# First queries by a cast load on GpSimd, bias differences from two loads, values by cast loads

## The chip, the cores and the metric

The kernel runs on one core of a Trainium2 chip. A core has a matmul engine (TensorE, PE in the profile; its weight loads are PEld), a vector engine (VectorE, DVE), a scalar engine (ScalarE, ACT), GpSimd (POOL) and a sync engine (SyncE, SP) that here only issues DMAs. Each engine works off its own instructions in order and waits on semaphores for the others. DMAs issued by SP and ACT go to hardware queues (q1 and q10 in the profile), those issued by POOL to a software queue (q0). A DMA that changes the type on its way (a cast load) is issued by POOL here. The metric is the time of one execution on the device in microseconds; lower is better.

## What is computed

Attention with a relative position bias, for 8 batch elements, 8 heads, 576 positions and head size 64, followed by a layer with two matmuls and a sine between them:

```python
scores = scale * np.matmul(q, k.transpose(0, 1, 3, 2))     # scale = 1/8
bias = bias_table[bucket]                                  # bucket of |i - j|, 32 buckets, 8 heads
scores = scores + bias.transpose(2, 0, 1)[None, :, :, :]
attn = softmax(scores)
x = np.matmul(attn, v)          # to (4608, 512), heads side by side
h = x @ w_in                    # (512, 2048)
g = h + np.sin(alpha * h) ** 2 / (alpha + 1e-09)
out = g @ w_out                 # (2048, 512)
```

Buckets of all distances of 128 and more share the last bucket. The bias table has 32 rows, one column a head.

## The kernel before

**Stages.** The batch elements are the index t, 0 to 7. For each t the kernel first does attention: score units on TensorE, exponentials on ScalarE, the bias as a product on VectorE, products with the values on TensorE, a normalisation on VectorE and a transpose into xT. Then comes the layer: matmuls with w_in, sines on ScalarE, squares on ScalarE or VectorE, g on VectorE, and matmuls with w_out, which are used later as fill between the score units of the next t. ScalarE loads a table of functions for the exponentials and another for the sines (ACT_TABLE_LOAD); the second load of the span marks the end of the first element's exponentials, the third the end of its sines.

**Bias.** The bias enters as a factor: exp(scores/8) is multiplied by exp(bias - last bias), with the last bucket's bias subtracted, so that far distances need no product. `less_last`, a 32x32 matrix that comes along in the constant `phi_x`, forms the differences by a product with the table `tabN` on TensorE (line 510). ScalarE takes the exponential (`tabE`, line 512), and `plan_table` spreads it over the distances by a product with `phi_sb`, copies the row to `e_sb` (line 595), writes it five times to DRAM (`e_dram`, line 596) and reads it back shifted by one element a partition as `m2r` (line 470) and `mhr` (line 477). The loads of `m2r` and `mhr` are issued by SP, in order, the first of them once `e_dram` has landed.

**Score units.** An attention element is four pairs of heads p, worked in two groups g. For t = 0 a pair has five units: four of kind A (128 keys by 512 queries and two heads, `ex` at line 678 with 128x1024 elements) and one of kind C (the last 64 keys of both heads, 128x576). Each takes two of TensorE's eight accumulation banks; three such pairs of banks are in use. For A units VectorE multiplies the part near the diagonal by `m2r` (line 703), for C units VectorE or GpSimd by `mhr` (line 687). Products with the values (`plan_av`) are groups of nine matmuls with one column more than the values, which gives the sum for the normalisation (lines 885 and 886). Its result is transposed by TensorE (line 910) or by a DMA, and copied to `xT`.

**First keys and queries.** For t = 0 keys and queries come from the inputs and are transposed by TensorE. Pair 0 comes by two SP loads in 32 bits (`nat0`, lines 489 and 490), is cast into `natb` by VectorE (keys, line 464), ScalarE and GpSimd (queries, lines 515 and 516), and takes six transposes of 96x128 each for keys and queries (line 550). Pairs 1 to 3 come by cast loads of GpSimd (`load_pair`, `nat1`) and take twelve transposes of 96x64 each (line 556). VectorE copies all of them to `kT` and `qT` (line 539), and GpSimd copies the last 64 keys to `kt` (line 581). For t = 1 all heads come by two cast loads (`loads2`, `nat2`), later elements from a staged copy by DMA transposes.

**First values.** Heads 0, 1 and 4 to 7 come by SP loads in 32 bits into the space of `w_out` (`load_v32`, line 416) and are cast by GpSimd (`cast_v`, line 419); heads 2 and 3 by cast loads (`load_vh`, line 411). The last 64 positions of all heads come by `load_vt`. The loads of `w_in` are issued by GpSimd behind `cast_v(4)`.

**Filler matmuls.** `warm` and `warm1` put matmuls on zeros (`zz`) onto TensorE, eight with 512 columns at the start, and shorter ones behind transposes and score units (`pad`) and in planned gaps. Their result is not used.

**Order.** The instructions ahead of `Plan` stand in the order of the code. Everything else is a task with its possible engines, an assumed cost on each, what it depends on, a priority, and in places a time before which it is not planned (the constants `T_...`). `Plan.run` places the tasks in assumed time before the launch and so writes each engine's order out; the chip then only waits on semaphores. A change of a constant can therefore move instructions far from it.

Of the kernel before, what the change touches and what calls it, by code (L numbers as in the profile page):

```python
# [209 lines left out]
WARM_END = 22.0  # L210
# [7 lines left out]
T_WI = 16.7  # L218
T_E = 5.9
T_CL = 20.5  # L220
T_FIRST = (5.2, 6.3)
T_PAIR = ((7.0, 7.4), (8.8, 9.4), (11.0, 11.6))
T_ACT = ()
T_M2 = (13.0, 14.5, 16.0, 16.0)
T_MH = 15.8
T_RST = 25.0
T_V0 = (7.5, 8.2, 8.9, 9.6)
T_VA = (10.5, 11.0)
T_VB = (16.3, 17.8, 18.3, 18.8)
T_AL = (20.0, 100)  # L230
# [4 lines left out]
NORM0 = 1200  # L235
SQ = {"ACT": 0.52, "DVE": 0.38}
T_V = ((15.5, 19.0), (50.0, 50.0))
T_TR1 = (36.5, 38.0)
T_W = (25.5, 30.5)
T_WO = (41.0, 43.5, 46.5, 49.5)  # L240
WARM0 = 8
WARM1 = 5
WARM_LAG = 0.3
WARM_GAP = 0.12
WARM_FROM = 7.3
# [19 lines left out]
def kernel(  # L265
# [41 lines left out]
    for x in range(EW - 1):  # L307
        phi_np[bt[abs(x - 255)], x] = 1.0
    last_np = np.eye(NB, dtype=np.float32)
    last_np[NB - 1] -= 1.0  # L310
    phi_h = nc.inline_tensor(np.concatenate([phi_np, last_np.view(np.float16)], axis=1), "phi_const")
# [24 lines left out]
    phi_x = sgl.tile([NB, EW + 2 * NB], F16, name="phi_sb")  # L336
    phi_sb, less_last = phi_x[:, 0:EW], phi_x[:, EW : EW + 2 * NB].bitcast(F32)
# [10 lines left out]
    N0 = 2 * 2 * SI * D  # L348
    nat0 = natx[0:SN, 0 : 2 * N0].bitcast(F32).rearrange("s (kq h x) -> s kq h x", kq=2, h=2)
    natb = natx[0:SN, 2 * N0 : 3 * N0].rearrange(  # L350
        "s (kq i two d) -> s kq i two d", kq=2, i=SI, two=2
    )
# [110 lines left out]
    def cast0(kq, eng):  # L463
        eng.tensor_copy(
            out=natb[:, kq], in_=nat0[:, kq].rearrange("s two (i d) -> s i two d", i=SI)
        )

# [15 lines left out]
    P_ = nc.gpsimd  # L483
    P_.memset(id_sb, 1.0)
# [4 lines left out]
    load_nat(nat0[:, 0], 0, 2, k[0], nc.sync)  # L489
    load_nat(nat0[:, 1], 0, 2, q[0], nc.sync)  # L490
    nc.scalar.dma_start(out=tabN, in_=bias_table)
    nc.scalar.dma_start(out=phi_x, in_=phi_h.ap())
    nc.scalar.dma_start(out=alphaN, in_=moe_alpha.rearrange("(f p) -> f p", p=128))
    load_v32(0)
    load_v32(1)
# [7 lines left out]
    load_pair(2)  # L503
    P_.tensor_copy(out=idf_sb, in_=id_sb[0:NF, 0:NF])
# [3 lines left out]
    for _ in range(WARM1):  # L508
        warm1(7, 192)
    full(pb[0:NB, 1, 0:H], less_last, tabN, True, True)  # L510
    warm1(7, 192)
    nc.scalar.activation(out=tabE, in_=pb[0:NB, 1, 0:H], func=AF.Exp)
    cast0(0, nc.vector)
    x0 = nat0[:, 1].rearrange("s two (i d) -> s i two d", i=SI)
    nc.scalar.activation(out=natb[:, 1, :, 0], in_=x0[:, :, 0], func=AF.Copy)
    P_.tensor_copy(out=natb[:, 1, :, 1], in_=x0[:, :, 1])

# [23 lines left out]
    def plan_tr(t, p, kq, pri, nb, deps=()):  # L541
# [3 lines left out]
        def mm(e):  # L545
            c.v = bank(b).bitcast(F16)
            for i in range(SI):
                x = i * SN
                if t == 0 and p == 0:
                    nc.tensor.transpose(  # L550
                        out=c.v[:, x : x + SN], in_=natb[:, kq, i], identity=id_sb[0:SN, 0:SN]
                    )
                    continue
                for z in range(2):
                    h = 2 * p - 2 + z if t == 0 else 2 * p + z
                    nc.tensor.transpose(
                        out=c.v[64 * z : 64 * z + 64, x : x + SN],
                        in_=(nat1 if t == 0 else nat2)[:, kq, h, D * i : D * i + D],
                        identity=id_sb[0:SN, 0:SN],
                    )  # L560
# [8 lines left out]
        if t == 0:  # L569
            m.pad = (256,) if p else (192,) * (5 if kq else 1)  # L570
        eng = {"DVE": 0.75, "ACT": 0.6}
        if t == 0:
            eng = {"ACT": 0.65} if p in T_ACT and kq else {"DVE": 0.75}
# [13 lines left out]
    def plan_table():  # L587
# [6 lines left out]
        def cp(e):  # L594
            nc.scalar.activation(out=e_sb, in_=bank(b)[0:H, 0:EW], func=AF.Copy)
            nc.scalar.dma_start(
# [11 lines left out]
        plan.add({"ACT": 1.0}, cp, [x], -1100, use=[b])  # L608
# [498 lines left out]
```

## Time and profile before

| | |
|---|---|
| median of 3 runs | 382.89 us (382.48 to 382.98) |
| profiled execution | 383.65 us |
| its span, first to last instruction | 381.8 us |
| mean granted TensorE clock | 0.991 |
| TensorE busy | 373.5 us, 98% of the span |
| ScalarE busy | 313.5 us, 82% |
| VectorE busy | 266.9 us, 70% |
| table load after the first element's exponentials | at 30.77 us |
| table load after the first element's sines | at 50.39 us |

The profile is of one execution, and times in it count from the start of its span. Durations below are from it; the median is of other executions of the same kernel. A row of the chain of waits has a start, a length, and an engine with what it writes and the line, or DMA with what it moves. A row of the timeline has a start, a duration, the engine, the line, the operation and its operands; for a DMA it is the time to issue it, and its landing is told apart. [...]

### The profile page before, as it was taken

The numbers are of one execution on the slowest core, as the hardware profiler recorded it, in microseconds if no ns is written. First come the engines' busy times: TensorE is split into PE (matmuls) and PEld (weight loads), VectorE is DVE, ScalarE is ACT, GpSimd is POOL, SyncE is SP. The second block draws the span as 40 slices with busy tenths as digits, with TensorE's granted clock in tenths as the row PEclk, the third lists the DMA queues.
The fourth block names the chain that finished last, engine by engine and source line by source line (L and its number), as shares of the span: only waits on it lengthen the run. The fifth ranks groups of instructions, "written<-read, shape, count | busy, mean of one in ns | idle before, by whom it ended". The sixth has DMA issues, their size and how long they took to land.

```text
span 381.8 us, 8975 instructions
## 1 busy us (share of the span) xinstructions
PE 373.5 (98%) x3578; PEld 204.2 (53%) x3578; DVE 266.9 (70%) x590; ACT 313.5 (82%) x432; POOL 92.9 (24%) x136
## 2 busy tenths in 40 slices
PE   8899999999999999999999999999999999999995
PEld 4365445654465445785564456544677456444442
DVE  4496976769676967697668867796769676999000
ACT  2978999869997999799987999699979997998111
POOL 7477350046000550037000900073005000000000
PEclk9979999999999999999999999999999999999999
DMA  9989999299912999279927991699629522000212
GB/s 170 177 160 196 203 154 134 56 162 116 89 53 74 151 120 121 79 130 113 137 60 123 103 165 44 105 147 139 78 75 155 60 53 74 6 2 1 77 63 82
DMA packets 148106, 40.16 MB, mean 105 GB/s; under 512 B 136200, under 2 KB 142432, under 8 KB 148064
## 3 DMA queue, kind: packets, MB, share of 16 engines
q0 software_dynamic: 96032, 17.67, 57.3%
q1 hardware_dynamic: 51856, 21.84, 25.1%
q8 instruction: 28, 0.46, 0.5%
q14 instruction: 14, 0.11, 0.1%
q10 hardware_dynamic: 176, 0.09, 0.1%
HBM read 37.73 MB, written 16.56 MB: 142 GB/s over the span
## 4 chain that ended last, share of the span: by engine, by line
PE 89%; ACT 5%; DMA 2%; DVE 2%; issue 1%; ACTq 0%; DVEq 0%; SPq 0%
PE pb L454 89%; ACT s L950 2%; DMA m2r<-e_dram 1%; ACT u L678 1%; DMA e_dram<-e_sb 1%; ACT sq L957 1%; PE pb L910 1%; ACT qT L537 0%; DVE u L703 0%; DVE xn L886 0%; DVE sq L959 0%; DVE outs L539 0%; DVE kT L539 0%; DVE g L964 0%; ACT xT L537 0%
## 5 line engine op out<-in xcount | busy, mean ns | idle before, releaser
L678 ACT ACTIVATE u<-pb 128x1024 f16<-128x1024 f32 (+1 forms) x174 | 152.7, 962 | 12.8 <-PE pb L454 12.0
L454 PE MATMUL pb<-w_out,g 128*128 128x512 f16 x576 | 138.9, 380 | 0.2 <-DVE outs L539 0.2
L454 PE MATMUL pb<-xT,w_in 128*128 128x512 f16 (+4 forms) x704 | 127.7, 340 | 0.0
L950 ACT ACTIVATE s<-pb,alphaT 128x512 f16<-128x512 f32 x144 | 92.9, 685 | 15.4 <-PE pb L454 15.2
L964 DVE SCALAR_TENSOR_TENSOR g<-sq,inv_a,pb 128x512 f16<-128x512 f16 x144 | 101.3, 743 | 3.8 <-ACT sq L957 2.3
L454 PEld LDWEIGHTS <-w_in 128*128 128x128 f16 x704 | 64.1, 98 | 55.9
L703 DVE TENSOR_TENSOR u<-u,m2r 128x512 f16<-128x512 f16 (+1 forms) x128 | 62.4, 497 | 35.0 <-ACT u L678 31.4
L454 PEld LDWEIGHTS <-g 128*128 128x128 f16 x576 | 53.0, 98 | 60.1 <-issue 8.1
L454 PEld LDWEIGHTS <-u 128*128 128x128 f16 x1404 | 55.5, 99 | 10.9 <-issue 3.2
L454 PE MATMUL pb<-v,u 128*128 128x65 f16 x1248 | 55.3, 195 | 0.2 <-DVE u L703 0.2
L399 POOL COPY kt<-kT 64x256 f16<-64x256 f16 x12 | 5.6, 464 | 182.9 <-DMA kT<-staged_k 182.7
L454 PE MATMUL pb<-qT,kT 64*128 64x64 f16 (+1 forms) x512 | 42.8, 288 | 0.4 <-ACT u L678 0.2
L959 DVE TENSOR_TENSOR sq<-s 128x512 f16<-128x512 f16 x81 | 34.3, 425 | 11.1 <-ACT s L950 10.2
L957 ACT ACTIVATE sq<-s 128x512 f16<-128x512 f16 x63 | 39.8, 631 | 0.9
L454 PE MATMUL pb<-vh,u 128*128 128x130 f16 x156 | 34.9, 224 | 0.0
L886 DVE TENSOR_TENSOR xn<-pb,rd 128x256 f16<-128x256 f32 (+1 forms) x64 | 30.9, 482 | 2.4 <-DVE rd L885 0.3
L537 ACT ACTIVATE outs<-pb 128x512 f32<-128x512 f32 x15 | 9.0, 597 | 28.1 <-PE pb L454 28.1
L454 PEld LDWEIGHTS <-kT 64*128 64x128 f16 x512 | 16.7, 94 | 24.5 <-issue 16.6
L404 POOL DMA_DIRECT2D v<-in_v_dram x28 | 24.8, 898 | 4.7 <-DMA nat<-in_q_dram 2.4
L1025 ACT ACT_TABLE_LOAD x15 | 19.2, 1283 | 0.3
L885 DVE RECIPROCAL rd<-pb 128x4 f32<-128x4 f32 (+1 forms) x64 | 11.9, 185 | 10.8 <-PE pb L454 9.7
L539 DVE COPY outs<-pb 128x512 f32<-128x512 f32 x21 | 14.5, 689 | 4.1 <-PE pb L454 4.0
(77 smaller groups left out, 168.7 us busy)
## 6 DMA issues: line engine op xcount, KB each, us to landing
out_dram<-outs SPq DMA_DIRECT2D x36, 256.0 KB, 2.3
v<-in_v_dram POOLq DMA_DIRECT2D x28, 128.0 KB, 4.4
staged_k<-in_k_dram POOLq DMA_DIRECT2D x6, 576.0 KB, 8.2
staged_q<-in_q_dram POOLq DMA_DIRECT2D x6, 576.0 KB, 12.0
w_in<-in_moe_w_in_dram POOLq DMA_DIRECT2D x4, 512.0 KB, 7.8
w_out<-in_moe_w_out_dram POOLq DMA_DIRECT2D x4, 512.0 KB, 15.1
xT<-xn SPq DMA_TRANSPOSE x60, 2.3
w_out<-in_v_dram SPq DMA_DIRECT2D x6, 128.0 KB, 4.8
```

Source lines behind the costliest of these rows:

```text
L404: nc.gpsimd.dma_start(out=vs[t % 2][:, c, :, 0:D], in_=vp[128 * c : 128 * c + 128],)
L454: nc.tensor.matmul(out=out, lhsT=lhsT, rhs=rhs, start=start, stop=stop)
L539: k_of(e).tensor_copy(out=o, in_=i)
L678: nc.scalar.activation(out=o, in_=x, func=AF.Exp, scale=0.125)
L703: nc.vector.tensor_tensor(out=io, in0=io, in1=m2[:, 2 * p : 2 * p + 2, x0 : x0 + hi - lo], op=ALU.mult)
L885: nc.vector.reciprocal(out=r, in_=x[:, :, :, D])
L886: nc.vector.tensor_tensor(out=xn.v[:, 0:nq].rearrange("p c (z d) -> p c z d", z=2), in0=x[:, :, :, 0:D], in1=r.unsqueeze(3).to_broadcast([ ...
L950: nc.scalar.activation(out=s16.v, in_=h.v, func=AF.Sin, scale=alphaT[:, f : f + 1])
L957: nc.scalar.activation(out=sq.v, in_=s16.v, func=AF.Square)
L959: k_of(e).tensor_tensor(out=sq.v, in0=s16.v, in1=s16.v, op=ALU.mult)
L964: nc.vector.scalar_tensor_tensor(out=gcell[b].v[:, f, :], in0=sq.v, scalar=inv_a[:, f : f + 1], in1=h.v, op0=ALU.mult, op1=ALU.add,)
L1025: nc.scalar.preload_act_table_set(name)
```

## The change

- The queries of pair 0 come by a cast load into `natq`, the first instruction of GpSimd, ahead of the identity matrix. They are transposed in twelve 96x64 pieces like the later pairs, without casts. The keys of pair 0 keep their SP load and VectorE's cast, now as the only cast. All three later pairs are loaded straight behind on GpSimd.
- The table's last row is loaded a second time, repeated over 32 partitions (`tabL`); VectorE subtracts, ahead of the key cast in its order. The constant holds `phi` alone, and the product with `less_last` and the five fillers ahead of it are gone. `phi` is now the first load on ScalarE's queue, `tabL` the second, `alphaN` the third; `tabN` is SP's second load.
- `e_dram` is written by a DMA of SP instead of ScalarE.
- The values of heads 0 to 3 all come by cast loads; `load_v32(0)`, `load_v32(1)` and their casts are gone.
- Copies of the queries of pairs 0 and 3 are ScalarE's (`T_ACT`), the first ahead of the first exponential, the second behind the seventh. The transpose of alpha stands behind the first score unit, and its three VectorE operations right behind.
- The multiply by `mhr` of pair 1 moves to VectorE, four copies of xT of the first element from ScalarE to VectorE. GpSimd's clearing of the second buffers moves behind the loads of `nat2` and `w_out`.
- With the planned times the order of score units, products and transposes of the first element changes: transposes of later pairs stand between the first score units, and the first product stands behind the eleventh score unit instead of the twelfth. There are 21 fillers instead of 40. From the second element on, the instructions are the same, in nearly the same order.

The core of the diff:

```diff
-WARM_END = 22.0
+WARM_END = 20.0
...
-T_E = 5.9
...
-T_FIRST = (5.2, 6.3)
-T_PAIR = ((7.0, 7.4), (8.8, 9.4), (11.0, 11.6))
-T_ACT = ()
-T_M2 = (13.0, 14.5, 16.0, 16.0)
-T_MH = 15.8
...
+T_E = 4.75
...
+T_FIRST = (5.0, 5.4)
+T_PAIR = ((7.4, 8.1), (8.8, 9.5), (10.2, 10.9))
+T_M2 = (11.8, 13.0, 14.4, 14.4)
+T_MH = 12.8
+T_ACT = (0, 3)
...
-WARM1 = 5
-WARM_LAG = 0.3
+WARM_LAG = 0.8
...
-    phi_h = nc.inline_tensor(np.concatenate([phi_np, last_np.view(np.float16)], axis=1), "phi_const")
+    phi_h = nc.inline_tensor(phi_np, "phi_const")
...
     P_ = nc.gpsimd
+    load_nat(natq, 0, 2, q[0], P_)
+    load_nat(nat0, 0, 2, k[0], nc.sync)
+    nc.scalar.dma_start(out=phi_sb, in_=phi_h.ap())
+    nc.sync.dma_start(out=tabN, in_=bias_table)
+    nc.scalar.dma_start(out=tabL, in_=bias_table[NB - 1 : NB, :].to_broadcast([NB, H]))
+    nc.scalar.dma_start(out=alphaN, in_=moe_alpha.rearrange("(f p) -> f p", p=128))
     P_.memset(id_sb, 1.0)
...
-    load_nat(nat0[:, 0], 0, 2, k[0], nc.sync)
-    load_nat(nat0[:, 1], 0, 2, q[0], nc.sync)
-    nc.scalar.dma_start(out=tabN, in_=bias_table)
-    nc.scalar.dma_start(out=phi_x, in_=phi_h.ap())
-    nc.scalar.dma_start(out=alphaN, in_=moe_alpha.rearrange("(f p) -> f p", p=128))
-    load_v32(0)
-    load_v32(1)
...
     load_pair(1)
     load_pair(2)
+    load_pair(3)
...
     warm(WARM0)
-    for _ in range(WARM1):
-        warm1(7, 192)
-    full(pb[0:NB, 1, 0:H], less_last, tabN, True, True)
-    warm1(7, 192)
-    nc.scalar.activation(out=tabE, in_=pb[0:NB, 1, 0:H], func=AF.Exp)
-    cast0(0, nc.vector)
-    x0 = nat0[:, 1].rearrange("s two (i d) -> s i two d", i=SI)
-    nc.scalar.activation(out=natb[:, 1, :, 0], in_=x0[:, :, 0], func=AF.Copy)
-    P_.tensor_copy(out=natb[:, 1, :, 1], in_=x0[:, :, 1])
+    nc.vector.tensor_tensor(out=tabD, in0=tabN, in1=tabL, op=ALU.subtract)
+    nc.scalar.activation(out=tabE, in_=tabD, func=AF.Exp)
+    nc.vector.tensor_copy(out=natb, in_=nat0.rearrange("s two (i d) -> s i two d", i=SI))
...
             nc.scalar.activation(out=e_sb, in_=bank(b)[0:H, 0:EW], func=AF.Copy)
-            nc.scalar.dma_start(
+            nc.sync.dma_start(
                 out=e_dram.ap()[:, 0:H].rearrange("r h x -> h r x"),
...
     def plan_v0():
-        plan.add({"POOL": 1.4}, lambda e: load_pair(3), [], -950, nb=5.8)
-        for i in range(2):
-            plan.add({"POOL": 0.45}, lambda e, i=i: cast_v(i), [], 9004 + i, nb=T_VA[i])
-        for i in range(4):
-            plan.add({"POOL": 0.7}, lambda e, i=i: load_vt(0, i) if i < 2 else load_vh(0, i),
-                     [], 9000 + i, nb=T_V0[i])
+        for i in range(6):
+            plan.add({"POOL": 0.7}, lambda e, i=i: load_vt(0, i) if i < 2 else load_vh(0, i - 2),
+                     [], 9000 + i, nb=T_V0 + 0.7 * i)
...
-                {"POOL": 0.6} if t == 0 and p else {"DVE": 0.19}, bd, [x], base + 10, nb=late, use=[ub])
+                {"POOL": 0.6} if t == 0 and p > 1 else {"DVE": 0.19}, bd, [x], base + 10, nb=late, use=[ub])
...
-        return [plan.add({"DVE": t_dve(n), "ACT": t_act(n) + 0.03}, put, [x], base + NORM_PRI,
-                         use=[tb])]
+        engs = {"DVE": t_dve(n) if t else 0.22, "ACT": t_act(n) + 0.03}
+        if t == 0 and 2 * p + w < 5:
+            del engs["ACT"]
+        return [plan.add(engs, put, [x], base + NORM_PRI, use=[tb])]
...
-                tr[(0, p + 1, kq)] = plan_tr(0, p + 1, kq, (150, 650, 5)[p], T_PAIR[p][kq])
+                tr[(0, p + 1, kq)] = plan_tr(0, p + 1, kq, (1, 2, 3)[p], T_PAIR[p][kq])
```

## The prediction

> **What bounds the kernel now.** I read the page first, then the chain of waits, then the first 50 us in the timeline, in the waits and in short windows.
>
> ```profile
> PE 373.5 (98%) x3578; PEld 204.2 (53%) x3578; DVE 266.9 (70%) x590; ACT 313.5 (82%) x432; POOL 92.9 (24%) x136
> PE 89%; ACT 5%; DMA 2%; DVE 2%; issue 1%; ACTq 0%; DVEq 0%; SPq 0%
> ```
>
> These are whole-span averages. The chain in order of time shows two parts. From 49.88 us on it is almost TensorE alone, and the change alters none of that work. Before that it passes through other things:
>
> ```profile
> 7.31 0.59 ACT e_sb L595
> ...
> 7.92 3.24 DMA e_dram<-e_sb
> ...
> 11.25 5.26 DMA m2r<-e_dram
> ...
> 16.61 0.43 DVE u L703
> 17.03 0.68 DVE kT L539
> 17.71 0.04 issue
> 17.75 6.14 PE pb L454 x56
> ...
> 49.88 5.65 PE pb L454 x57
> ```
>
> Columns are start, length and what. The bias row e_sb goes out to DRAM and comes back as m2r; VectorE's first multiply by m2r stands ahead of the last key copy in VectorE's order, so the last pair's scores wait for m2r. The waits between 8 and 31 us say the same (total, times, longest):
>
> ```profile
> ACT u L678 <- PE pb L454: 4.1, 3, 2.0
> DVE u L703 <- DMA m2r<-e_dram: 2.8, 1, 2.8
> PE pb L454 <- DVE kT L539: 1.6, 1, 1.6
> ```
>
> ScalarE's 20 exponentials of the first batch element run from 9.42 to 30.77, idle for 0.08+0.57+0.01+2.04+0.33 = 3.03 us of it. Windows of 3.4 us (engine, busy us; the last three columns are granted clock, DMA share, GB/s):
>
> ```profile
> 0.60:4.00 3.40, 2.74 (x7) 1.04 (x8) 1.35 (x9) 1.28 (x1) 3.00 (x6) 1.00 0.57 171
> 4.00:7.40 3.40, 3.40 (x24) 1.90 (x22) 1.32 (x2) 0.67 (x3) 2.33 (x5) 1.00 1.16 182
> 14.30:17.70 3.40, 1.68 (x26) 0.82 (x20) 1.09 (x3) 3.40 (x5) 0.00 (x0) 0.95 0.84 195
> 17.70:21.10 3.40, 3.35 (x29) 1.76 (x29) 3.40 (x7) 2.47 (x3) 2.47 (x6) 0.50 0.85 184
> 21.10:24.50 3.40, 3.40 (x44) 2.61 (x41) 3.04 (x7) 1.38 (x3) 3.40 (x7) 0.54 0.78 131
> ```
>
> After TensorE sat idle for half of 14.3 to 17.7, its clock is 0.50 until about 24.5.
>
> **The change, part by part.** The rows are of one execution: 383.65 us, span 381.8 and 1.85 around it; the median of the runs is 382.89. I work out a shift of the early part and take it from both. A shift carries through: TensorE has no room after 49.88 and runs the same matmuls.
>
> *Bias path.* Removed: the 0.27 us product at 5.59 that makes the differences, with 5 fillers ahead of it. Added: a second load of 1 KB (last row, repeated), a VectorE subtraction, and an issue on SP in place of ScalarE for e_dram. The two small loads are second on their queues, issued at 1.27. The same load first on its queue took 2.49; the one that was second (phi) took 3.76: they land between 3.76 and 5.03. I take 4.4, halfway, since they are as small as the first and as late as the second. Subtraction at most 0.17 (the small VectorE rows are 0.06 to 0.19), exponential 0.17: 4.75. The eight 512-column fillers ahead in TensorE's order end at 1.26 + 8 x 0.43 = 4.7, which hides an earlier landing. Product with phi 0.57: e_sb starts at 5.4 instead of 7.31, -1.9 (-2.0 to -1.3 over the bounds). Then 0.59, 3.24 and 5.26 as in the rows: m2r at 14.65 instead of 16.51. The issue on SP costs nothing: the loads of m2r behind it wait for it anyway. The two transfers' own times are the doubt. Loads of values from 3.77 to 5.42 and the small loads from 2.49 to 4.10 bound them: 12.4 to 15.6, of which the early end brings nothing (the next path is late then) and the late end leaves -0.9. I keep the rows themselves: the same transfers, with the engines' share at 1.15 to 1.33 now; two loads of 512 small packets leave this stretch on SP, and the two that replace them come later on GpSimd.
>
> *First queries and keys.* The key cast (0.59) now waits behind the subtraction: 4.5 to 5.1 instead of 3.98 to 4.57. Its six transposes stand behind the product, 5.4 to 6.1 (0.69), and the key copy ends at 6.85 instead of 7.41. Queries: the first load that GpSimd issues took 0.81 to issue, the next 0.64. No row shows a cast load with nothing ahead of it at the start; nearest are the later cast loads that met a quiet queue, 3.77 to 5.42, and at the far end those behind others, 6.57 to 7.61. I take 4.6, the middle of the near ones: 5.4. It has until 6.15, when the key transposes and one filler are done; every us beyond is late one for one, at worst 2.3. Gone are the casts of queries on GpSimd (0.50) and ScalarE (0.51). Twelve transposes at the slow rate (0.06 each), ScalarE's copy 0.67, four fillers beside it, scores 0.39: the first exponential at 8.1 instead of 9.42, -1.3. The six other pair loads are issued 0.7 later for the first (2.3) and 0.5 to 1.1 earlier for the third; the first used to land at 8.07 through 1,024 small packets of values, now gone, and its keys are now first needed at about 9. Alpha's transpose and three VectorE operations (0.84) move from 26.12 to about 8.6, under the wait for the first pair: nothing; without that cover they would put off the key copy by 0.84.
>
> *Values.* Heads 0 to 3 come by cast loads in GpSimd's order after the first two key tails: issued at about 10.8, 11.5, 12.8, 13.5. At 3.77 to 5.42 they land at 14.6 to 16.9 and 16.6 to 18.9. The products of pair 0 would start at about 17.2 (19.81 now, less the 1.9 and a copy of 0.67 that leaves VectorE's order before them), those of pair 1 two score units and a product later, about 19: no cost taken; if such a load takes 6.57, as the first keys did behind others, head 1 lands at 18.1, 0.9 late (a rival). Six casts on GpSimd become four. The cast that holds up the w_in loads waits for a load behind m2r on SP, so w_in, now first issued at 20.35, moves with m2r; so does the stream up to w_out.
>
> *VectorE and ScalarE between m2r and 31 us.* VectorE gives up one query copy (0.67) and alpha (0.84) and takes four copies of xT (0.2 each) and one multiply by mhr (0.17): 0.5 less. ScalarE gives up three xT copies (0.3 each) and takes two query copies (0.53 of its time each), both before the stall. I count neither: they shorten idle time as much as work. In the sine stage ScalarE has 16 sines and 12 others either way (6 squares, 6 copies now; 4 and 8 then), 15.9 us from 34.53 to 50.39; VectorE gets two squares more and two copies fewer. No change.
>
> *Sum.* The products of pair 0 need m2r (-1.9). In TensorE's order they stand behind the eleventh score unit, and the remaining score units stand between them, each waiting for an exponential to free its banks (-1.3). The end of the first batch element takes part of each; I take -1.5, between the two. 382.89 - 1.5 = 381.4, or 382.15 in the profiled execution.
>
> [...] The half clock ended only after 21.1:24.5, which was busy 3.40 of 3.40, not after 17.7:21.1 with 3.35. The start is similar: five 192-column fillers take 0.58 in all at 7.47, while one takes 0.36 on its own at 6.41, after a window with 3.40. The change drops 19 of 40 fillers, and its order has small gaps between 4.7 and 7.6 (for the table, the key cast, the queries). [...]
>
> **Rivals.** *Clock lost (slower).* If TensorE stays at half clock past about 14 us and on through the second dip, the score units cost 0.53 instead of 0.33 and twelve transposes 0.75 instead of 0.38: 11 x 0.2 + 6 x 0.37 = 4.4 us before 15 us, of which idle TensorE time takes about 2. Then -1.5 + 2.4 = +0.9: 383.8. For it: the gaps above. Against: at half clock the work itself closes the gaps, so a full window may come by 10.8, which costs next to nothing. *Clock kept.* If the idle stretch before m2r is short enough that the clock stays up, products of nine cost 0.40 instead of 0.55 and scores 0.2 less: 6 x 0.15 + 4 x 0.2 = 1.7 us of the 6.14, some of it VectorE's then; I take 1.3: 380.1. Against: from about 13 on the score units come only as exponentials free their banks, one in 0.9 us, and the products wait until about 17: nearly the same dip. *Traffic.* m2r hardly moves, because all pair loads are queued sooner and take the engines' time: -0.4, 382.5. For it: the share of 1.15 to 1.33 in this stretch; against: 1,024 packets fewer on SP. *Values late*: the 0.9 above is lost, -0.6: 382.3.
>
> **Chances.** Forecast 0.42 (380.8 to 382.1 by itself), clock kept 0.20, values late 0.12, traffic 0.14, clock lost 0.12. Faster by over 0.2% (about 0.77 us, what a measurement of this kernel can tell) is below 382.12: nearly all of the forecast, all of clock kept, a third of values late: 0.65. Slower is clock lost, above 383.66: 0.13 with a tail. The rest, 0.22, is the same. The range reaches from clock kept with its half us (379.6) to just short of clock lost (383.3).
>
> **What would show it.** In the profile after: e_sb near 5.4, m2r landing near 14.65, first exponential near 8.1, table load after the exponentials near 29.0 instead of 30.77, the second one near 48.9 instead of 50.39, and the same TensorE tail. Wrong if queries land after 6.5, if m2r takes well over 5.3, if TensorE waits for a value load at 16 to 19, or if the clock column reads 0.5 beyond one stretch of about 7 us.

## The result, and the profile after

The change makes the kernel slower: 384.20 us (median of 20 runs, 382.9 to 387.09) against 382.48 for the kernel before (20 runs, 381.6 to 383.43), a ratio of 1.0057 of the mean times, 95% interval [1.0039, 1.0075]. Measured again with 12 and 29 runs it was 1.0024 [1.0011, 1.0037]. The sign is sure; the two intervals together reach from 0.1% to 0.75%, and they do not overlap. The forecast was 381.4, and a gain.

The profiled execution took 384.47 us with a span of 382.8. The page's busy times and its chain by engine, after:

```profile
PE 373.9 (98%) x3563; PEld 202.9 (53%) x3563; DVE 266.4 (70%) x594; ACT 314.0 (82%) x429; POOL 93.4 (24%) x135
PE 87%; DMA 7%; POOL 2%; ACT 1%; SPq 1%; issue 1%; DVE 0%; ACTq 0%; DVEq 0%; POOLq 0%
```

No engine has more work than before; the chain has 7% of DMA where it had 2%. The chain in order of time (start, length, what) says which:

```profile
5.63 0.60 ACT e_sb L580
6.24 5.04 DMA e_dram<-e_sb
...
14.84 7.27 DMA w_out<-in_v_dram
22.16 0.41 POOL v L415
22.57 1.30 POOL w_in L431 x2
...
29.88 12.49 DMA nat<-in_q_dram
42.41 0.45 PE pb L541 x12
```

"w_out<-in_v_dram" are the 32-bit value loads of heads 4 to 7. e_sb starts 1.7 us sooner than before, and still the chain arrives at 42.4 us at a transfer: nat2's queries. The waits between 30 and 52 us (total, times, longest):

```profile
PEld L541 <- DMA nat<-in_q_dram: 2.4, 1, 2.4
PE pb L541 <- DMA nat<-in_q_dram: 1.9, 1, 1.9
ACT qT L522 <- PE pb L541: 1.3, 1, 1.3
```

TensorE stands 2 us in front of the transposes of nat2, and ScalarE behind it. ScalarE's two table loads in the timeline are the milestones:

```profile
29.80 1.28 ACT L1014 ACT_TABLE_LOAD   x1
51.15 1.28 ACT L1014 ACT_TABLE_LOAD   x1
```

The exponentials end 1.0 us sooner than in the profile before (30.77), the sines 0.8 later (50.39). In this execution the loss arises in the sine stage, 21.35 us long instead of 19.62.

### The profile page after: what moved, and what is told of

Same layout as the page of the kernel before. It is cut to its first block, busy times and chain, and to the rows that moved or that the text cites. A ratio compares the mean times of both kernels' runs of the same rounds, so it can differ in the third digit from the quotient of the medians.

```text
span 382.8 us, 8938 instructions
## 1 busy us (share of the span) xinstructions
PE 373.9 (98%) x3563; PEld 202.9 (53%) x3563; DVE 266.4 (70%) x594; ACT 314.0 (82%) x429; POOL 93.4 (24%) x135
## 4 chain that ended last, share of the span: by engine, by line
PE 87%; DMA 7%; POOL 2%; ACT 1%; SPq 1%; issue 1%; DVE 0%; ACTq 0%; DVEq 0%; POOLq 0%
PE pb L450 86%; DMA nat<-in_q_dram 3%; DMA w_out<-in_v_dram 2%; DMA e_dram<-e_sb 1%; ACT u L660 1%; DMA tabL<-in_bias_table_dram 1%; PE pb L541 1%; PE pb L895 1%; POOL w_in L431 1%; SPq L461 0%; SPq L468 0%; POOL u L669 0%; POOL v L415 0%; POOL nat L672 0%; POOL nat L425 0%
## 5 line engine op out<-in xcount | busy, mean ns | idle before, releaser
L450 PEld LDWEIGHTS <-u 128*128 128x128 f16 x1404 | 54.4, 98 | 11.4 <-issue 3.4
L450 PE MATMUL pb<-v,u 128*128 128x65 f16 x1248 | 54.4, 194 | 0.6 <-ACT u L660 0.3
L450 PE MATMUL pb<-qT,kT 64*128 64x64 f16 (+1 forms) x512 | 44.1, 293 | 0.2
L948 DVE TENSOR_TENSOR sq<-s 128x512 f16<-128x512 f16 x83 | 35.4, 431 | 11.6 <-ACT s L939 10.7
L946 ACT ACTIVATE sq<-s 128x512 f16<-128x512 f16 x61 | 38.3, 628 | 0.9
```

Of the source, the lines that this page charges most:

```text
L450: nc.tensor.matmul(out=out, lhsT=lhsT, rhs=rhs, start=start, stop=stop)
L946: nc.scalar.activation(out=sq.v, in_=s16.v, func=AF.Square)
L948: k_of(e).tensor_tensor(out=sq.v, in0=s16.v, in1=s16.v, op=ALU.mult)
```

## The experiments

Ratios are to the kernel before, with 95% intervals. The theories that the expectations name: **S**, the stream of w_in, nat2 and w_out on q0 starts late, because GpSimd waits for value loads; **O**, the transposes of nat2 (constant `T_TR1`, which the change moves from 36.5 and 38.0 to 33.5 and 36.0) stand too early in TensorE's order; **C**, the half clock at the start costs the time; **P**, the profile that the prediction read was a rare case; **W**, TensorE's wait brings a half clock of its own; **T**, e_dram waits in the DMA engines behind the pair loads.

### Parts of the changed kernel taken back

**w_in ahead of value casts (a_win).**

```diff
-        x = plan.add({"POOL": 1.4}, lambda e: load_w_in16(0, (0, 2)), [], 9006, nb=T_WI, after=vdone[0:2])
+        x = plan.add({"POOL": 1.4}, lambda e: load_w_in16(0, (0, 2)), [], 9003, nb=T_WI)
```

> The changed kernel, with one edit: the first two w_in loads stand in GpSimd's order ahead of the casts of the values of heads 4 to 7, not behind two of them. Nothing else moves on any engine. Theory S (the stream is late: GpSimd waits 4.2 us for a 32-bit value load that takes 7.06 to 7.27 us, and everything behind that wait on GpSimd's queue lands late): the first w_in is issued at about 17.3 instead of 22.51, the stream lands some 3 to 5 us sooner, the queries of nat2 at 38 to 39.5 instead of 42.37, TensorE's wait of 2.4 us for them is gone, the table load after the sines comes near 49.3 instead of 51.15, and the ratio to the kernel before falls from 1.0057 to about 0.998 to 1.001. Theory C (what is lost is the half clock that TensorE keeps until 20.5): the time stays at 1.004 to 1.007, since clock and first exponentials are the same. Theory O (the transposes of nat2 stand too early in TensorE's order): also about 1.000, so S and O are told apart by the next runs.

1.0015 [0.9995, 1.0035]. The edit did less than the expectation says: w_in moved ahead of the second cast only, and was issued at 21.86. It tells nothing on S; a_win2 below does.

**Values of heads 0 and 1 as before (a_v).**

```diff
+    load_v32(0); load_v32(1)
...
+        [plan.add({"POOL": 0.45}, lambda e, i=i: cast_v(i), [], 9004 + i, nb=(10.5, 11.0)[i]) for i in range(2)]
-        for i in range(6):
-            plan.add({"POOL": 0.7}, lambda e, i=i: load_vt(0, i) if i < 2 else load_vh(0, i - 2), ...
+        for i in range(4):
+            plan.add({"POOL": 0.7}, lambda e, i=i: load_vt(0, i) if i < 2 else load_vh(0, i), ...
```

> The changed kernel, with the values of heads 0 and 1 as in the kernel before: two 32-bit loads of SP behind the table's load, two casts of GpSimd in place of two cast loads. TensorE, VectorE and ScalarE keep their order. Theory S: with two cast loads fewer beside them the 32-bit loads of heads 4 to 7 take 4.4 to 5 us again instead of 7.06 to 7.27, the first w_in is issued at about 20.3, the queries of nat2 land near 40.5, the table load after the sines comes at 49.3 to 49.8 and the ratio falls to 0.998 to 1.001. If it is the first loads that suffer instead (SP's two value loads back beside the pair loads), the second pair's keys land 1 us later and half of that is lost: 1.002. Theory C: no change, 1.004 to 1.007.

1.0017 [1.0005, 1.003]. The value loads of heads 4 and 5 landed at 21.18 and 21.64, w_in was issued at 22.25: not the sooner start that S expected.

**The transposes of nat2 later (a_tr).**

```diff
-T_TR1 = (33.5, 36.0)
+T_TR1 = (36.5, 38.0)
```

> The changed kernel, with T_TR1 as before (36.5 and 38.0 instead of 33.5 and 36.0): the transposes of nat2's keys and queries stand later between the w_in matmuls, and some sines and squares stand ahead of the copies of kT and qT. The loads are the same. Theory O (the order is at fault, not the stream): TensorE has matmuls to do until 42.37, does not wait for nat2, the table load after the sines comes at 49.5 to 50, ratio 1.000 to 1.002. Theory S in its strict form: the late nat2 is only met a little later, and w_out is late as well (52.65 instead of 50.85), so at most half of the 2.4 us comes back: 1.003 to 1.005. Theory C: 1.004 to 1.007.

1.0005 [0.9993, 1.0017]: no loss is left that is clear of noise, though w_in was issued at 22.09 and nat2 landed at 41.87, nearly as late as in the changed kernel. The wait for nat2 between 30 and 52 us fell from 2.4 to 0.4 us, and the second table load came at 48.97 instead of 51.15:

```profile
PEld L541 <- DMA nat<-in_q_dram: 0.4, 1, 0.4
```

O, against S in its strict form. The interval meets those of the other runs with the early place (a_win and a_v, 1.0015 and 1.0017), and its median, 383.24 us, is above the 382.52 of the kernel before beside it, so this run alone does not settle how much comes back; b_tr below tries the place by itself. The wait also depends on when TensorE gets there. In the profiles of a_win, a_v, a_fill and a_ed the clock was at half for 3.4 to 10.2 us between 16 and 27 us, the exponentials ended at 30.40 to 31.07, the wait with the early place was only 0.4 to 0.7 us, and the second table load came at 50.42 to 50.56.

**More fillers (a_fill).**

```diff
-WARM_LAG = 0.8
+WARM_LAG = 0.3
...
-    warm(WARM0)
+    warm(WARM0); [warm1(7, 192) for _ in range(3)]
...
-            m.pad = (256,) if p else (192,) * (4 if kq else 1)
+            m.pad = (256,) if p else (192,) * (5 if kq else 1)
```

> The changed kernel with 13 fillers more: three of 192 columns ahead of the product with phi, one more behind the first query transposes, and nine in gaps (WARM_LAG 0.3 as before). The order of all else is the same but for the two squares that change places. Theory C: TensorE gets its full clock by about 7 to 9 us as in the kernel before, twelve transposes take 0.38 instead of 0.62 and a score unit 0.33 instead of 0.54, the first exponentials follow each other at 0.92 instead of 1.16, the table load after the exponentials comes near 28.8 instead of 29.80, and the ratio falls to about 1.000 to 1.002; the single times scatter less than 382.9 to 387.1. Theory S: the start may be quicker, but w_in is still issued at about 22.5 and nat2 lands at 42.4, so the table load after the sines stays near 51 and the ratio at 1.004 to 1.007.

1.003 [1.0017, 1.0044]. Full clock from 5.64, but half clock once more from 19.3 to 22.7, and no gain beyond what the kernel's second measurement has anyway.

**e_dram on ScalarE's queue (a_ed).**

```diff
-            nc.sync.dma_start(
+            nc.scalar.dma_start(
                 out=e_dram.ap()[:, 0:H].rearrange("r h x -> h r x"),
```

> The changed kernel with one edit: e_dram is issued by ScalarE as before, not by SP. e_dram took 5.04 us in the changed kernel and 3.24 before. If the queue is what makes it slow: 3.2 to 3.6 us, m2r lands near 12.8 to 13.5, 1 us or more sooner; the time moves by at most 0.2%, since the sines wait for nat2 anyway. If it is the traffic (six pair loads are queued on the 16 DMA engines by 6.56, four of them before): 4.6 to 5.2 us again and the same m2r, ratio 1.003 to 1.007 as without the edit.

1.0033 [1.0011, 1.0054]; e_dram took 4.59 us. Not the queue.

### Both kernels once more

> The kernel before, unchanged, profiled once more. The profile that the prediction was made from has a mean granted clock of 0.991 and takes 383.65 us, but none of the 35 timed runs of the kernel before that went along with the first four experiments is below 0.996, 27 of them are at 0.999 or 1.000, and their median is 382.52. Theory P (the profile showed a rare case): this one has a clock of 0.998 or more, no half clock between 17 and 24 us, the table load after the exponentials at about 29.3 to 30 instead of 30.77, the one after the sines at about 49 to 49.5 instead of 50.39, and a time near 382.5. Its rival (the profile was typical and the half clock costs nothing): half clock from 17 on again, table loads within 0.3 us of 30.77 and 50.39.

The kernel before, profiled again, took 382.17 us, clock 1.000. Its table loads:

```profile
28.02 1.28 ACT L1025 ACT_TABLE_LOAD   x1
48.52 1.28 ACT L1025 ACT_TABLE_LOAD   x1
```

Theory P holds. The half clock from 17.4 to 24.2, which the prediction's chain rests on, is not there. It takes 0.009 from the mean clock; of the 139 timed runs of the kernel before that went along with the experiments one is at 0.992 or below (383.69 us), 123 are at 0.998 or more (median 382.61). This execution of the kernel before ends its sines at 48.5: where the prediction put the changed kernel (48.9).

> The changed kernel, unchanged, again. In its first 20 runs the clock told three groups: 0.999 and 1.000 (382.9 to 384.8), 0.982 to 0.991 (383.3 to 385.3) and 0.995 or 0.996 (383.9 to 387.1). One half-clock stretch of 3.4 us takes 0.0045 from the mean, so the third group has exactly one. Theory W (TensorE's wait of 2.4 us for the queries of nat2 brings that one stretch at 40 to 47 us, in the stage that waits for TensorE): the same three groups again, median 383.7 to 384.5, ratio 1.003 to 1.006; if the profile falls into the third group, its half clock lies between 40 and 48 us, if into the second, between 15 and 28. Its rival (the scatter has nothing to do with nat2): the third group's half clock lies before 30 us.

The changed kernel again: 1.0024, and its profile (384.23 us) fell into the third group. First exponential at 7.16, first table load at 27.98, but the second at 50.92. Beside the second profile of before, which like it has full clock from about 4.5 on, the first exponential comes 1.7 us sooner (8.84 there), but the exponentials end at the same time (28.02 there): on the way TensorE waits 1.4 us for a normalisation of VectorE, and ScalarE then 2.6 us for a score unit. nat2's queries land at 40.52 in both. Windows of 3.41 us around nat2, counted on from the clock steps of each execution (busy us of PE, PEld, DVE, ACT, POOL, then granted clock, mean busy share of the 16 DMA engines, GB/s), first of this execution, then of the first profile after:

```profile
35.31:38.72 3.41, 3.36 (x26) 1.31 (x24) 3.39 (x7) 3.41 (x7) 1.27 (x2) 1.00 1.31 207
38.72:42.13 3.41, 1.57 (x26) 0.84 (x28) 2.42 (x4) 1.73 (x4) 0.87 (x1) 1.00 1.23 195
42.13:45.54 3.41, 3.41 (x31) 1.64 (x25) 1.22 (x3) 2.40 (x4) 0.63 (x1) 0.50 1.23 194
```

```profile
37.61:41.02 3.41, 2.87 (x24) 1.11 (x21) 3.38 (x7) 3.41 (x7) 0.95 (x2) 1.00 1.30 204
41.02:44.43 3.41, 2.02 (x41) 1.23 (x42) 1.94 (x4) 1.69 (x3) 0.88 (x1) 1.00 1.20 186
```

The wait for nat2 is 2.4 us in both. In a_look it falls into one window: TensorE is busy 1.57 us of it and the next window runs at half clock, in the stage in which ScalarE's sines wait 3.1 us for TensorE. In the first profile after it is split over two, busy 2.87 and 2.02, and the clock stays. The busy time alone does not decide it: in the first profile of before the window from 13.96 to 17.37 is also busy 2.02 us, and half clock follows. In the traces of these two first profiles the steps of the clock stand whole multiples of 3.41 us apart: in the first profile of before it is full for 10.24 us from 7.13, half for 6.83 and full again for 358.40 (3, 2 and 105 of them), in the first profile after full for 361.81 (106). That what TensorE does in one such stretch sets the clock of the next is the author's reading. Such a half-clock window may be behind the runs of up to 387 us: in the first 20, the seven whose mean clock fits exactly one (0.995 or 0.996) have a median of 386.22, the eight at 0.999 or more 383.86. In the second measurement three runs at 0.996 and five at 0.998 or more stand at 384.23 and 383.17, so the price of the window isn't one number. The mean clock does not count a half clock at the start: the trace's clock records begin with the first full clock (at 7.13 in the first profile of before, at 20.54 in the first profile after), and ahead of it the clock column reads 1.00. So the runs of one group can still differ in their start.

### The suspected parts alone, on the kernel before

**T_TR1 alone (b_tr).**

```diff
-T_TR1 = (36.5, 38.0)
+T_TR1 = (33.5, 36.0)
```

> The kernel before with T_TR1 of the changed kernel alone (33.5 and 36.0): the first transposes of nat2 stand behind 33 w_in matmuls instead of 37, 24 in a row. Loads and the start are as before. Theory O (this place makes TensorE wait for nat2, 2.4 us in the changed kernel, and drops its clock for one or two stretches of 3.4 us in some runs): nat2's queries land at 40.5, TensorE waits 1 to 2.5 us for them, the ratio is 1.002 to 1.005, and some runs have a mean clock of 0.995 or 0.996. Theory S (the place does no harm as long as the stream is in time): 0.999 to 1.001.

1.0062 [1.004, 1.0084]: this one constant brings as much as the whole change. Loads, exponentials and first table load (28.09) are as in the second profile of before; nat2's queries land at 40.73. The wait for them between 30 and 52 us, here and in the second profile of before:

```profile
PEld L556 <- DMA nat<-in_q_dram: 2.3, 1, 2.3
```

```profile
PEld L556 <- DMA nat<-in_q_dram: 1.2, 1, 1.2
```

The window of the wait and the next:

```profile
38.42:41.83 3.41, 1.23 (x26) 0.67 (x19) 3.04 (x6) 2.71 (x5) 1.62 (x2) 1.00 1.27 205
41.83:45.24 3.41, 3.41 (x31) 1.62 (x30) 0.38 (x1) 1.79 (x4) 0.69 (x2) 0.50 1.21 195
```

The second table load comes at 53.08 instead of 48.52. The half clock is not needed for the loss: the three of the six runs with a mean clock of 0.998 or more took 383.77 to 384.65 us, the other three 384.94 to 385.80, against a median of 382.44 before. S, which said that the place does no harm while the stream is in time, has fallen.

**The three data paths alone (b_all).** The cast load of the first queries, the subtraction with `tabL`, the cast loads of values 0 and 1, e_dram on ScalarE, three fillers instead of five at the start, all constants of the plan as before but one:

```diff
-T_E = 5.9
+T_E = 4.75
...
+    load_nat(natq, 0, 2, q[0], P_)
...
+    nc.sync.dma_start(out=tabL, in_=bias_table[NB - 1 : NB, :].to_broadcast([NB, H]))
...
+    nc.vector.tensor_tensor(out=tabD, in0=tabN, in1=tabL, op=ALU.subtract)
```

> The kernel before with the three data paths of the change and nothing else: first queries by a cast load (natq), bias differences by a load of the last row (tabL, SP's second load here) and a subtraction, values of heads 0 and 1 by cast loads; the times of the plan stay as before but T_E, which goes to 4.75, and VectorE keeps both copies and alpha stays late. Theory O+S (the data paths are worth something, the plan around them loses it): the first exponential comes at 8 to 8.4, m2r lands near 14.5, and the ratio is 0.996 to 0.999. Theory S in its strict form (the value loads delay heads 4 to 7 and so w_in whatever the plan is): nat2 lands later than 41.5 and the ratio is 1.000 to 1.004. Theory P (the dip that the prediction counted on is not there in most executions, so there is little to gain): 0.999 to 1.001.

0.9999 [0.9979, 1.0019]: neither a gain nor a loss within 0.2%, where the forecast's 1.5 us would be 0.4%. The chains of the kernel before (second profile) and of this one:

```profile
6.87 0.59 ACT e_sb L595
7.49 3.89 DMA e_dram<-e_sb
...
14.77 5.67 DMA w_out<-in_v_dram
...
20.89 1.39 POOL w_in L435 x2
```

```profile
5.74 0.60 ACT e_sb L595
6.36 4.92 DMA e_dram<-e_sb
...
14.68 5.66 DMA w_out<-in_v_dram
...
20.79 1.43 POOL w_in L435 x2
```

e_sb starts 1.13 us sooner, and e_dram takes 1.03 longer. It lands at the same moment, and all behind it stays: SP's loads, the cast, w_in, the span (380.2 both).

### w_in sooner

**a_win2, a_tr_win2, b_win.** The first w_in loads ahead of all casts of heads 4 to 7: in the changed kernel, in a_tr, and in the kernel before.

```diff
-... load_w_in16(0, (0, 2)), [], 9006, nb=T_WI, after=vdone[0:2])
+... load_w_in16(0, (0, 2)), [], 9003, nb=15.9)
```

> The changed kernel with the first two w_in loads ahead of all four casts of values (the first such run had moved them ahead of the second cast only, so that GpSimd still waited for the first one and w_in was issued at 21.86). Nothing else moves but on GpSimd. Theory S (the stream of w_in, nat2 and w_out on q0 sets the end of the early part): the first w_in is issued at about 17.3, the queries of nat2 land at 37 to 39.5, w_out's last at 48 to 49.5 instead of 52.65, TensorE does not wait for nat2, the ratio is 0.994 to 0.999. Theory O (the place of the transposes of nat2 alone): the same, as they land ahead of their place. A price that would speak against both: w_in takes the engines from the 32-bit value loads of heads 4 to 7, these land at 23 to 25 instead of 21.4 to 22.9, the products of pairs 2 and 3 wait, the table load after the exponentials comes 1 to 2 us later, and the ratio stays at 1.000 to 1.004.

> The changed kernel with both edits: w_in ahead of all casts of values, and T_TR1 as before. Theory S+O: as with w_in alone, or up to 0.1% better, 0.994 to 0.998, and no run with a half clock beyond 30 us. If the late transposes now hold up the second element's scores instead (nat2 is there early and they stand late): 0.001 to 0.002 worse than w_in alone.

> The kernel before with the same edit: the first two w_in loads behind the last keys' copies and ahead of the multiply by mhr and all casts of heads 4 to 7. Theory S: w_in is issued at 16.5 to 18.5 instead of 20.4 to 20.8, the last w_out lands 2 us sooner, and the ratio is 0.995 to 0.998. If the start is bound by the exponentials and sines and not by the stream: 0.999 to 1.001. If the values of heads 4 to 7 pay for it: 1.000 to 1.004.

1.0085 [1.0054, 1.0115], 1.0101 [1.007, 1.0132] and 1.011 [1.0087, 1.0133]. w_in was issued at about 17 in all three, and the price named in the first expectation came: the last value load landed at 27.43, 28.81 and 28.8, against 22.85 in the first profile after and 21.77 in the second one before. GpSimd's wait for it in the first of them:

```profile
POOL v L415 <- DMA w_out<-in_v_dram: 7.8, 2, 5.4
```

Behind that cast stand GpSimd's multiplies by mhr and the second half of w_in. It was wrong to expect a gain from an earlier start of the stream whatever else is being loaded. The price is not paid in every execution: two of the 12 runs of a_win2 took 382.13 and 382.67 us, two of a_tr_win2 382.44 and 383.11, all others of the two 385.69 or more; no profile shows one of these four.

### What holds e_dram, and the chain behind it

**c_p3, c_p23.** The three data paths alone (b_all), with the loads of pair 3, or of pairs 2 and 3, issued after e_dram.

```diff
-        plan.add({"POOL": 1.4}, lambda e: load_pair(3), [], -950, nb=5.8)
+        plan.add({"POOL": 1.4}, lambda e: load_pair(3), [], -950, nb=8.6)
```

> The kernel before with the three data paths (as in the run that gave 0.9999), and the two loads of pair 3 issued behind the loads of the last 64 values, at about 8.6 us, not at 5.3 and 6.0. Nothing else moves. Theory T (e_dram waits in the DMA engines behind the pair loads that are queued before it): e_dram takes 3.4 to 4.3 us instead of 4.92, m2r and all behind it come 0.6 to 1.5 us sooner, the first w_in at 19.3 to 20.2 instead of 20.8, and the ratio is 0.996 to 0.999. Rival (e_dram's time is its own, or that of pairs 1 and 2): 4.7 to 5.1 us, ratio 0.999 to 1.002.

> As before it, and the loads of pair 2 also later, at about 7.2 us. Theory T: only pair 1's loads are beside e_dram when it is issued at 6.4, it takes 2.5 to 3.5 us and lands near 9.3; m2r at 12 to 13.5. The keys of pair 2 land at 11 to 12 instead of 9.0, so the score units of pair 2 and the time are an open matter: 0.997 to 1.003. Rival: e_dram 4.5 us or more all the same.

e_dram took 3.33 us in the first; in the second m2r was issued 2.06 after e_dram, so it took that at most. Theory T: with six, four and two pair loads ahead, 4.92, 3.33 and 2.06, each in one execution and issued at 6.2 to 6.5. The times are 1.0007 [0.9994, 1.002] and 1.0046 [1.003, 1.0063]. The chain of the first says where the gain went:

```profile
6.50 3.33 DMA e_dram<-e_sb
...
13.07 8.39 DMA w_out<-in_v_dram
...
22.16 1.43 POOL w_in L435 x2
```

The value load is issued 1.6 us sooner and lands 1.1 later: beside it now run the pair and value loads that came later (landing at 14.97, and at 17.3 to 21.85). In the second, TensorE waited 0.9 us for pair 2's queries and 1.4 for pair 3's keys, and its clock was at half from 15.2 to 22.1.

**c_vsp, c_p3_vsp, d_tr, d_vsp.** On SP the value loads of heads 4 to 7 ahead of the last m2r load: with the data paths; with c_p3; with the data paths and T_TR1 at 37.5 and 39.0; alone on the kernel before.

```diff
-            load_m2r(nc.sync, 4, H, 4)
             for h in range(4, H):
                 load_v32(h)
+            load_m2r(nc.sync, 4, H, 4)
```

> The kernel before with the three data paths, and on SP the four value loads of heads 4 to 7 ahead of the last m2r load (heads 4 to 7) instead of behind it. Nothing else moves. If the chain of SP loads sets when w_in starts and w_in sets the end of the early part: the value loads are issued 0.5 us sooner and land 0.5 to 1.5 us sooner, the first w_in is issued at 19.3 to 20.3, the last w_out lands 0.5 to 1 us sooner, ratio 0.997 to 0.999. If the last m2r load is then late for VectorE's multiplies of pair 2 (it lands at 21 to 22 instead of 19.85): 1.000 to 1.003.

> Both: pair 3's loads behind the last values, and the value loads ahead of the last m2r load. If e_dram, the value loads and w_in are one chain to the end, the gains of both add up: first w_in at 18.5 to 19.5, ratio 0.995 to 0.998. If the stream is not the limit any more once it starts before about 20, the ratio stays at 0.998 to 1.000.

> The kernel before with the three data paths, the value loads of heads 4 to 7 ahead of the last m2r load on SP, and T_TR1 at 37.5 and 39.0: the first transposes of nat2 behind 41 w_in matmuls instead of 37 (33 made the kernel before 0.62% slower). If a wait of TensorE for nat2 in front of the sines costs time here too: no such wait, the table load after the sines at 48 to 49.3, ratio 0.996 to 0.998, and no run with a half clock near 42 us. If the place as before is late enough: 0.998 to 1.000, as without the edit. If later transposes hold up the second element: 1.000 to 1.003.

> The kernel before with SP's order alone: the value loads of heads 4 to 7 ahead of the last m2r load. If that order, and not the data paths, made the 0.9987: 0.997 to 0.9995, the first w_in 0.3 to 0.8 us sooner. If it was chance or needs the data paths: 0.9995 to 1.002.

0.9987 [0.9973, 1.0001], 1.0007 [0.9993, 1.0021], 0.9992 [0.9977, 1.0008], 0.9991 [0.9975, 1.0008]. In c_p3_vsp w_in is issued at 19.17 and the last w_out lands at 49.23, against 20.84 and 51.17 in the second profile of before, and the time is no better: its chain now goes through the last m2r load (landing at 21.95), for which VectorE waits 2.2 us. T_TR1 later than in the kernel before brought nothing more. None of the four is shown to be faster than the kernel before.

## Why the prediction was wrong, point by point

- **The sine stage** ("No change") is the step behind the loss. It counted ScalarE's and VectorE's instructions, but neither looked at the place of nat2's transposes in TensorE's order nor asked when nat2 lands. The first transposes of its queries stand behind 44 w_in matmuls in the kernel before and in a_tr, behind 40 in the changed kernel, behind 36 in b_tr; four take 0.97 us. That constant alone makes 1.0062, and with its old value the changed kernel is at 1.0005. It is one of the planned times that the change moves, and no term of the sum stood for it.
- **The gain of 1.5 us** in the sum failed by itself. With the old place of nat2's transposes the changed kernel is at 1.0005 [0.9993, 1.0017] and not at 0.996, and the data paths alone are at 0.9999. The points on e_dram, on the base and on the clock say what is known of where it went.
- **"I keep the rows themselves"** for e_dram (3.24) and m2r (5.26) was wrong in both: 5.04 and 3.17, each outside its bounds (2.49 to 4.10 and 3.77 to 5.42). m2r landed at 14.47, forecast 14.65 (its own terms give 14.60), by two errors that cancel: luck. In the kernel before, too, all six pair loads are issued ahead of e_dram. In its five profiles with this start (before, b_look, b_tr, b_win, d_vsp) e_dram was issued at 6.94 to 7.92 and landed at 11.16 to 12.05; the one issued last landed first. So the row of 3.24 could not be carried to an earlier start. The rival *traffic* was right that the pair loads hold a transfer up (e_dram took at most 2.06 us, 3.33 and 4.92 with two, four and six of them ahead), but took it for m2r and priced it at a gain of 0.4; the data paths alone gave none that could be measured.
- **"w_in ... moves with m2r; so does the stream"** failed: m2r came 2.0 us sooner, w_in 2.2 later (22.51). That delay moves nat2 and w_out; with T_TR1 as before it costs nothing that could be measured (a_tr). It is not even needed for the wait: in a_look w_in was issued at 20.61, and TensorE waited for nat2 just as long.
- **The base.** The sum was made on an execution with two windows of half clock and "taken from both" that execution and the median. The half clock that follows the stall from 16 us on is absent from nearly all timed runs of the kernel before, and in its second profile the stall itself is smaller: m2r lands at 15.09 instead of 16.51, and ScalarE waits 1.8 us for score units between 7 and 31 us instead of 4.1. The median of 382.89 against the profile's 383.65 was noted and not asked about.
- **The small steps were right.** tabE was done at 4.96 (forecast 4.75), e_sb started at 5.63 (5.4), the queries landed at 5.22 (5.4), the first exponential came at 8.36 (8.1), alpha cost nothing, and from the second table load on the span is 331.65 us (331.4 in the profile before, 331.7 in the second): there a shift does carry through.
- **Values late.** They landed at 16.41 to 21.91, later than the forecast 14.6 to 18.9, but the waits of TensorE name none of them: no cost shown.
- **Clock lost.** In the first profile after, TensorE stayed at half clock until 20.5, where the trace's clock records begin, as this rival said, although the windows from 7.4 to 17.6 were busy 3.40 of 3.40 us by the profile; the prediction had counted such a full window against the rival. In the first profile of before the half clock ended after a window busy 3.42 of 3.42 us (20.78 to 24.20); that one is enough no run shows, and here three were not. Its transposes of the pairs (duration min/median/max in ns), in that profile and in a_look, where the clock was full from 4.58:

```profile
L541 PE MATMUL pb<-id_sb,nat x72: 277/281/290, 9.7 to 16.9; 96*64 96x96 f16 x72
```

```profile
L541 PE MATMUL pb<-id_sb,nat x60: 205/207/231, 8.9 to 12.4; 96*64 96x96 f16 x60
```

  The second dip, on which its price of 2.4 us rested, did not follow. The first table load came 1.8 us later than in a_look, and the second at nearly the same time, 51.15 and 50.92: in these two profiles the place of nat2 takes back what the start gains. Many timed runs of the changed kernel lose more clock than one half-clock window of 3.41 us takes (0.0045): its mean clock is 0.991 or lower in 7 of 32 runs, that of the kernel before in one of 139; where in the run, no profile shows. Fillers (a_fill) didn't bring the time to that of before, but their profile has a half clock of its own. So this rival did not make the loss by itself, as a_tr keeps the same start and has none that is clear of noise; what the lost clock costs, and whether it hides a gain, stays open: no profile shows full clock from about 5 us on together with the changed start and the old place of nat2's transposes.

Shown by runs: that T_TR1 alone costs the kernel before about as much as the change does, that with its old value the changed kernel has no loss clear of noise, that the data paths alone bring neither gain nor loss beyond 0.2%, and that e_dram's time falls with the number of pair loads ahead of it. Argued only: that the one half-clock window after the wait is what makes the slowest runs; it was seen in two profiles, a_look and b_tr. Open: what the half clock at the start costs, and why the two measurements of the changed kernel differ by more than their intervals.

## What to carry to other kernels

When a change moves planned times, read the order of the busiest engine through all stages, and set each moved instruction against the landing of what it reads: here one wait of 2.3 us in front of a full engine cost more (0.62%, b_tr) than the whole change was to gain (0.4%). Before a sum is built on a stall in a profile, see whether the stall belongs to the kernel or to that execution; a median well under the profiled time is a sign (here 382.89 against 383.65). A transfer that leaves sooner may land no sooner, so its duration cannot be carried over from another start: here e_dram left 1.13 us sooner and took 1.03 longer with six loads queued ahead of it (b_all against b_look), and took 3.33 us with four (c_p3).

## What the runs showed of the hardware

- A 40 KB write to DRAM took 4.92 us, 3.33, and at most 2.06, with six, four and two loads of 144 KB queued ahead on GpSimd's queue, though it was on another queue itself; in the other executions with the changed first loads it took 4.59 to 5.82 with six ahead and 3.66 with four. With six loads ahead it landed at 11.28 (b_all), and the last of them at 11.52.
- A 32-bit value load of 128 KB took 7.27 us in the first profile after, where two cast loads of values were issued within 0.5 us of it (14.37 and 15.10, the load at 14.84), 5.58 in a_look, where they had been issued by 12.50, and 8.39 in c_p3, where a pair load landing at 14.97 ran beside it too. Beside the first w_in loads the last one took 10.3 to 12.9 us (a_win2, b_win, a_tr_win2).
- A TensorE window 46% or 36% busy (1.57 and 1.23 of 3.41 us) was followed by half clock. One 59% busy (2.02) was not in the first profile after, and was in the first profile before; one 53% busy (1.81, from 18.24 in a_look) was not, and one 66% busy (2.25, from 12.80 in c_p3_vsp) was. From 53% to 66% the busy time does not tell it. The same 2.4 us wait was followed by half clock where it fell into one window (a_look), and not where it was split over two (the first profile after).
- Three windows of TensorE rows that were busy throughout (3.40 of 3.40 us, from 7.4 to 17.6 in the first profile after) did not end the half clock of the start; it ended at 20.54, in a_look at 4.58.
